# Attention in blocks of 64 queries with multiplied masks, interleaved by hand with the FFN of the chunk before

## The chip, the cores and the metric

The kernel runs on one core of a Trainium2 chip. The time is device microseconds of one execution, from a median of several runs. TensorE multiplies matrices into PSUM, VectorE (DVE) and ScalarE (ACT) read PSUM and SBUF, GpSimd (POOL) works on SBUF and issues the DMAs that cast float32 to bfloat16, SyncE (SP) issues plain DMAs.

## The reference

Eight batches, eight heads, 576 positions, head width 64. Attention is local (a query sees keys at most 32 away), and eight positions `global_idx` are global: they see all and are seen by all. The 4608 tokens of width 512 then go through a gated FFN of width 1536 with a gated residual:

```python
scores = scale * np.matmul(q, k.transpose(0, 1, 3, 2))
mask = np.abs(pos[:, None] - pos[None, :]) <= window
mask = mask | is_global[:, None] | is_global[None, :]
attn = softmax(np.where(mask, scores, -1e9))
x = np.matmul(attn, v)                      # tokens x 512
g, val = x @ w_gate, x @ w_val
ffn_out = (gelu(g) * val) @ w_out
return x + sigmoid(x @ w_res) * ffn_out
```

## The kernel before

One batch of attention is a stage of the main loop (L370). `load_batch` (L175) fetches q, k and v of the next batch in 18 casting DMAs of 96 rows on GpSimd's queue and 24 small ones for the global rows, whose addresses come from registers that all engines load at the start (L93). `transpose_batch` (L208) turns q and k with TensorE, so that a head's width lies on partitions, and ScalarE copies them out with the halos.

Per head, `qk_exp_head` (L234) computes scores of six key blocks: 96 keys and eight global keys on partitions, 160 queries and eight global queries on columns. For each block a first matmul adds the mask from `biasm` through the identity (L244, 128 rows), a second adds k times q (L246, 64 rows); then come two Exps. `av_head` (L253) multiplies with v, which carries a column of ones, so that row 64 of `nd` is the denominator. ScalarE copies numerators and denominators out.

`normalize_batch` (L273) runs after all heads of a batch: two reciprocals over 616 columns (L278), for each head two matmuls that broadcast the reciprocal over partitions (L287, L290), and three multiplies into `xt` and `xgt` (the global queries).

The FFN goes over nine chunks of 512 tokens. `piece_ff` (L309) makes one of 12 blocks of 128 FFN columns: four gate matmuls, four value matmuls, a Tanh that stands for the gelu, and two VectorE products into `ht`. `piece_st` (L328) makes 128 tokens of the output: 12 matmuls with `wo_t`, four with `wr_t`, four through the identity to bring x back in token order (L342), a Tanh, two VectorE operations and a store. The pieces wait in a list, and the loop takes one behind each head's scores and one behind each head's values (L381 to L387), so a chunk is interleaved with the attention of the next batch. What is left of the list is run before `normalize_batch`.

After the last chunk the 64 global tokens go through an FFN of their own (L407 to L439), and eight stores write them over their rows of the output (L440).

Of the kernel before, what the change touches and what calls it, by code (L numbers as in the profile page):

```python
# [8 lines left out]
_DEBUG_DUMP = False  # L9
# [5 lines left out]
AX = mybir.AxisListType  # L15
# [3 lines left out]
def kernel(  # L19
# [27 lines left out]
    PADQ = 32
    QW = PADQ + S + 32
    NDW = QW + SIDE
    NXC = NDW - PADQ  # L50
    NBIAS = -120.0
    NP = H // 2
    SHALF = 3 * BCOL
    VG = D + 2

    def sbase(kb):
        return BCOL * kb if kb < 3 else 512 + BCOL * (kb - 3)

    pieces = []
    bounds = sorted(set([BLK * kb for kb in range(KB)]  # L60
                        + [BLK * kb + WIN for kb in range(KB)] + [512, QW]))
    for i in range(len(bounds) - 1):
        c0, c1 = bounds[i], bounds[i + 1]
        if c0 >= QW:
            break
        c1 = min(c1, QW)
        kbs = [kb for kb in range(KB) if BLK * kb <= c0 and BLK * kb + WIN >= c1]
        assert kbs, (c0, c1)
        pieces.append((c0, c1, kbs))

    const = ctx.enter_context(tc.tile_pool(name="const", bufs=1))
    stage = ctx.enter_context(tc.tile_pool(name="stage", bufs=2))
    headp = ctx.enter_context(tc.tile_pool(name="headp", bufs=2))
    nump = ctx.enter_context(tc.tile_pool(name="nump", bufs=10))
    moep = ctx.enter_context(tc.tile_pool(name="moep", bufs=2))
    outp = ctx.enter_context(tc.tile_pool(name="outp", bufs=2))
    smallp = ctx.enter_context(tc.tile_pool(name="smallp", bufs=1))

    ps1 = ctx.enter_context(tc.tile_pool(name="ps1", bufs=6, space=bass.MemoryType.PSUM))
    psB = ctx.enter_context(tc.tile_pool(name="psB", bufs=1, space=bass.MemoryType.PSUM))  # L80

    ident = const.tile([128, 128], BF16, name="ident")
# [3 lines left out]
    ones64 = const.tile([128, 64], BF16, name="ones64")  # L86
    nc.vector.memset(ones64, 1.0)

    g32 = global_idx.bitcast(I32)
    gvals = []  # L90
    for i in range(NG):
        gap = bass.AP(tensor=g32.tensor, offset=g32.offset + 2 * i, ap=[[0, 1], [1, 1]])
        gvals.append(nc.values_load(gap))  # L93
    gsb = const.tile([1, NG], I32, name="gsb")
    nc.sync.dma_start(gsb, bass.AP(tensor=g32.tensor, offset=g32.offset, ap=[[0, 1], [2, NG]]))
    gf = const.tile([1, NG], F32, name="gf")
    nc.vector.tensor_copy(gf, gsb)
    gb32 = const.tile([32, NG], F32, name="gb32")
    nc.gpsimd.partition_broadcast(gb32, gf)
    diag8 = const.tile([8, NG], F32, name="diag8")  # L100
    nc.gpsimd.memset(diag8, 0.0)
    nc.gpsimd.affine_select(out=diag8, in_=diag8, pattern=[[-1, NG]], channel_multiplier=1, base=0,
                            compare_op=ALU.not_equal, fill=1.0)
    dtmp = const.tile([8, NG], F32, name="dtmp")
    nc.vector.tensor_tensor(dtmp, gb32[0:8, :], diag8, ALU.mult)
    gp8 = const.tile([8, 1], F32, name="gp8")
    nc.vector.tensor_reduce(gp8, dtmp, axis=AX.X, op=ALU.add)

    iota_i = const.tile([32, WIN], I32, name="iota_i")
    nc.gpsimd.iota(iota_i, pattern=[[1, WIN]], base=0, channel_multiplier=0)  # L110
    iotac = const.tile([32, WIN], F32, name="iotac")
    nc.vector.tensor_copy(iotac, iota_i)

    exc = const.tile([32, BCOL], F32, name="exc")
    nc.vector.memset(exc, 0.0)
    nc.vector.memset(exc[0:NG, 32:128], 1.0)

    bandf = const.tile([BLK, BCOL], F32, name="bandf")
    nc.gpsimd.memset(bandf, 0.0)
    nc.gpsimd.affine_select(out=bandf[:, 0:WIN], in_=bandf[:, 0:WIN], pattern=[[1, WIN]],  # L120
                            channel_multiplier=-1, base=0, compare_op=ALU.is_ge, fill=NBIAS)
    nc.gpsimd.affine_select(out=bandf[:, 0:WIN], in_=bandf[:, 0:WIN], pattern=[[-1, WIN]],
                            channel_multiplier=1, base=64, compare_op=ALU.is_ge, fill=NBIAS)
# [246 lines left out]
    for b in range(B):  # L370
# [19 lines left out]
        while pending:  # L390
            pending.pop(0)()
# [82 lines left out]
```

## Time and profile before

| | |
|---|---|
| median of three runs | 736.1 us (735.87 to 736.11) |
| span of the profiled execution (its time is not listed otherwise) | 729.6 us |
| TensorE busy | 85% |
| VectorE busy | 52% |
| ScalarE busy | 41% |
| GpSimd busy | 29% |
| mean granted TensorE clock | 0.916 of 2.4 GHz |

A busy TensorE is not TensorE at its peak: a matmul's recorded duration overlaps the next, and how fast the engine goes is read from start to start. Times in the rows are microseconds from the start of the span; in the lists of groups the mean is in nanoseconds.

### The profile page before, as it was taken

The numbers are of one execution on the slowest core, as the hardware profiler recorded it, in microseconds if no ns is written. First come the engines' busy times: TensorE is split into PE (matmuls) and PEld (weight loads), VectorE is DVE, ScalarE is ACT, GpSimd is POOL, SyncE is SP. The second block draws the span as 40 slices with busy tenths as digits, with TensorE's granted clock in tenths as the row PEclk, the third lists the DMA queues.
The fourth block names the chain that finished last, engine by engine and source line by source line (L and its number), as shares of the span: only waits on it lengthen the run. The fifth ranks groups of instructions, "written<-read, shape, count | busy, mean of one in ns | idle before, by whom it ended". The sixth has DMA issues, their size and how long they took to land.

```text
span 729.6 us, 11619 instructions
## 1 busy us (share of the span) xinstructions
PE 619.2 (85%) x4516; PEld 326.9 (45%) x4516; DVE 378.4 (52%) x647; ACT 301.8 (41%) x574; POOL 214.0 (29%) x353
## 2 busy tenths in 40 slices
PE   0009948998999899989999899989998999799991
PEld 0005534554555455544554455544554455244450
DVE  5702074485565636553654566355636362784740
ACT  0005445553655255525553455345544553132320
POOL 2853489804900590048003820260000000000000
PEclk9999999999799969995999599958996899799997
DMA  0909959906820691067304660240000000001010
GB/s 6 93 1 186 176 34 93 67 1 82 60 17 1 91 60 8 1 89 49 22 1 66 53 41 1 55 38 1 1 30 30 1 1 30 30 0 59 1 59 7
DMA packets 127558, 29.92 MB, mean 41 GB/s; under 512 B 119760, under 2 KB 121808, under 8 KB 127504
## 3 DMA queue, kind: packets, MB, share of 16 engines
q0 software_dynamic: 122176, 19.62, 35.4%
q1 hardware_dynamic: 5328, 9.57, 3.6%
q8 instruction: 35, 0.57, 0.3%
q14 instruction: 19, 0.16, 0.1%
HBM read 39.19 MB, written 9.57 MB: 67 GB/s over the span
## 4 chain that ended last, share of the span: by engine, by line
PE 46%; issue 28%; POOL 12%; DVE 6%; DMA 4%; POOLq 2%; ACT 1%; DVEq 0%
PE g_ps L316 10%; PE v_ps L320 9%; PE f_ps L334 7%; PE s_h L246 5%; PE s_h L244 5%; DMA wr_t<-in_moe_w_res_dram 4%; POOL ks_t L186 3%; POOL qs_t L184 3%; PE nd L259 3%; PE r_ps L338 2%; DVE xt L292 2%; POOL vt L188 2%; DVE rden L278 2%; PE pq L216 1%; PE pk L230 1%
## 5 line engine op out<-in xcount | busy, mean ns | idle before, releaser
L324 DVE SCALAR_TENSOR_TENSOR ht<-tsb,g_ps 128x512 bf16<-128x512 bf16 x108 | 73.1, 683 | 147.5 <-ACT tsb L323 147.3
L316 PE MATMUL g_ps<-xt,wg_t 128*128 128x512 bf16 x432 | 120.0, 402 | 0.3 <-DVE xt L292 0.3
L320 PE MATMUL v_ps<-xt,wv_t 128*128 128x512 bf16 x432 | 117.7, 397 | 0.0
L244 PE MATMUL s_h<-biasm,ident 128*128 128x168 bf16 x384 | 102.3, 266 | 0.0
L188 POOL DMA_DIRECT2D vt<-in_v_dram x48 | 37.1, 779 | 221.7 <-PE nd L264 214.1
L246 PE MATMUL s_h<-qte,kt 64*128 64x168 bf16 x384 | 101.0, 263 | 0.0
L334 PE MATMUL f_ps<-wo_t,ht 128*128 128x512 bf16 x432 | 99.2, 379 | 0.0
L323 ACT ACTIVATE tsb<-g_ps 128x512 bf16<-128x512 f32 x108 | 64.8, 600 | 60.1 <-PE g_ps L316 59.3
L278 DVE RECIPROCAL rden<-denb 97x616 bf16<-97x616 f32 x16 | 64.0, 4003 | 40.6 <-ACT denb L270 40.6
L325 DVE SCALAR_TENSOR_TENSOR ht<-ht,v_ps 128x512 bf16<-128x512 bf16 x108 | 73.5, 686 | 10.1 <-PE v_ps L320 1.9
L347 DVE SCALAR_TENSOR_TENSOR prb<-rsb,f_ps 128x512 f32<-128x512 bf16 x36 | 24.4, 676 | 94.2 <-ACT rsb L345 94.2
L267 ACT CAST numsb<-nd 64x616 bf16<-64x616 f32 x64 | 42.7, 667 | 68.5 <-PE nd L264 68.5
L216 PE MATMUL pq<-ident,qs_t 96*128 96x96 bf16 (+1 forms) x192 | 21.8, 281 | 57.1 <-DMA qs_t<-in_q_dram 54.7
L320 PEld LDWEIGHTS <-wv_t 128*128 128x128 bf16 x432 | 44.2, 102 | 56.9 <-issue 10.3
L218 ACT COPY qte<-pq 128x576 bf16<-128x576 bf16 x32 | 23.0, 719 | 111.2 <-PE pq L216 111.2
L334 PEld LDWEIGHTS <-ht 128*128 128x128 bf16 x432 | 40.0, 98 | 43.9 <-DVE ht L325 0.4
L345 ACT ACTIVATE rsb<-r_ps 128x512 bf16<-128x512 f32 x36 | 21.5, 598 | 91.5 <-PE r_ps L338 91.5
L246 PEld LDWEIGHTS <-kt 64*128 64x128 bf16 x384 | 36.4, 95 | 48.8 <-issue 15.0
L249 ACT ACTIVATE pt<-s_h 128x504 bf16<-128x504 f32 x64 | 39.6, 619 | 44.4 <-PE s_h L246 44.3
L259 PEld LDWEIGHTS <-vt 128*65 128x65 bf16 x1152 | 51.6, 121 | 13.3 <-issue 2.5
L259 PE MATMUL nd<-pt,vt 128*65 128x64 bf16 (+2 forms) x1152 | 54.1, 198 | 2.8 <-ACT denb L270 2.8
L244 PEld LDWEIGHTS <-ident 128*128 128x128 bf16 x384 | 38.4, 100 | 38.5 <-issue 1.5
(89 smaller groups left out, 777.2 us busy)
## 6 DMA issues: line engine op xcount, KB each, us to landing
out_dram<-ob SPq DMA_DIRECT2D x36, 256.0 KB
qs_t<-in_q_dram POOLq DMA_DIRECT2D x48, 96.0 KB, 3.7
ks_t<-in_k_dram POOLq DMA_DIRECT2D x48, 96.0 KB, 3.8
vt<-in_v_dram POOLq DMA_DIRECT2D x48, 96.0 KB, 4.2
wg_t<-in_moe_w_gate_dram POOLq DMA_DIRECT2D x1, 1536.0 KB, 10.6
wv_t<-in_moe_w_val_dram POOLq DMA_DIRECT2D x1, 1536.0 KB, 18.2
wo_t<-in_moe_w_out_dram POOLq DMA_DIRECT2D x1, 1536.0 KB, 24.9
qs_t<-in_q_dram POOLq DMA_DIRECT2D x64, 1.0 KB, 1.8
```

Source lines behind the costliest of these rows:

```text
L188: nc.gpsimd.dma_start(vt_t[0:BLK, kb, :, 0:D], vb[BLK * kb:BLK * kb + BLK])
L244: nc.tensor.matmul(sh[0:128, cb:cb + BCOL], ident, biasm[kb][0:128, 0:BCOL], start=True, stop=False)
L246: nc.tensor.matmul(sh[0:128, cb:cb + BCOL], kt[hb:hb + 64, kb, 0:128], qte[hb:hb + 64, kb, 0:BCOL], start=False, stop=True)
L259: nc.tensor.matmul(nd[0:D + 1, c0:c1], vt_t[:, kb, h, 0:D + 1], pt[:, cb + r0:cb + r0 + (c1 - c0)], start=(ii == 0), stop=(ii == len(kbs) ...
L267: nc.scalar.copy(numsb[0:D, :], nd[0:D, PADQ:NDW])
L278: nc.vector.reciprocal(rdt[0:97, :], denb_tiles[gi2][0:97, :])
L316: nc.tensor.matmul(g_ps, wg_t[:, kt2, 128 * j:128 * j + 128], xt[kt2][:, t0:t0 + 512], start=(kt2 == 0), stop=(kt2 == NKT - 1))
L320: nc.tensor.matmul(v_ps, wv_t[:, kt2, 128 * j:128 * j + 128], xt[kt2][:, t0:t0 + 512], start=(kt2 == 0), stop=(kt2 == NKT - 1))
L323: nc.scalar.activation(tsb, g_ps, ACTF.Tanh, bias=0.0, scale=0.851)
L324: nc.vector.scalar_tensor_tensor(ht[:, j, :], tsb, 1.0, g_ps, ALU.add, ALU.mult)
L325: nc.vector.scalar_tensor_tensor(ht[:, j, :], ht[:, j, :], 0.5, v_ps, ALU.mult, ALU.mult)
L334: nc.tensor.matmul(f_ps, ht[:, kt2, 128 * st:128 * st + 128], wo_t[:, kt2, :], start=(kt2 == 0), stop=(kt2 == NFF - 1))
```

## The change

The kernel is rewritten in an order fixed by hand. The 72 windows of 64 queries (nine per batch) are taken in chunks of eight, 512 tokens, so that attention and FFN chunks are the same tokens. The core, with the setup of constants left out:

```diff
+    psm = ctx.enter_context(tc.tile_pool(name="psm", bufs=4, space=bass.MemoryType.PSUM))
+    pss = ctx.enter_context(tc.tile_pool(name="pss", bufs=2, space=bass.MemoryType.PSUM))
+    psn = ctx.enter_context(tc.tile_pool(name="psn", bufs=1, space=bass.MemoryType.PSUM))
+    ctx.enter_context(tc.manual_schedule())
...
+    def load_qk(b):
+        for src, dst in ((q, q_st), (k, k_st)):
+            for r in range(NQT):
+                n = min(128, S - 128 * r)
+                nc.gpsimd.dma_start(dst[0:n, r, :].rearrange("p (h d) -> p h d", d=D),
+                                    src[b].rearrange("h s d -> s h d")[128 * r:128 * r + n])
...
+    def prep_pair(b, p, what):
+        src = q_st if what == "q" else k_st
+        ps = pss.tile([128, S], BF16, name=f"t{what}", tag="sc")
+        for r in range(NQT):
+            n = min(128, S - 128 * r)
+            nc.tensor.transpose(ps[:, 128 * r:128 * r + n], src[0:n, r, 128 * p:128 * p + 128], ident[0:n, 0:n])
+        if what == "q":
+            nc.scalar.copy(qt[b % 2][:, p, :], ps)
+        else:
+            nc.vector.tensor_copy(kt[b % 2][:, p, 32:32 + S], ps)
+    def prep_qz(b, p0, p1):
+        for u in range(2):
+            nc.vector.tensor_copy(qz[b % 2][64 * u:64 * u + 64, p0:p1, u, :],
+                                  qt[b % 2][64 * u:64 * u + 64, p0:p1, :])
+    def scores(c, quad, p):
+        sc = pss.tile([128, 4, 2, 64], F32, name="sc", tag="sc")
+        for n in range(4):
+            b, i = divmod(CH * c + 4 * quad + n, NW)
+            nc.tensor.matmul(sc[:, n, :, :], kt[b % 2][:, p, 64 * i:64 * i + 128],
+                             qz[b % 2][:, p, :, 64 * i:64 * i + 64], start=True, stop=True)
+        mine = view(pt, 0, 128, (2 * p * CH + 4 * quad) * 128, [[128, 4], [CH * 128, 2], [1, 64]])
+        nc.scalar.activation(mine, sc, ACTF.Exp, bias=0.0, scale=SCALE)
+        i0 = (CH * c + 4 * quad) % NW
+        nc.vector.tensor_tensor(mine, mine, view(maskw, 0, 128, 64 * i0, [[64, 4], [0, 2], [1, 64]]), ALU.mult)
+    def values(c, t):
+        nd = psn.tile([128, 2, 512], F32, name="nd", tag="nd")
...
+        for hf in range(2):
+            for n, (b, c0) in enumerate(parts):
+                nc.tensor.matmul(nd[:, hf, 0:HV], gt[b % 2][:, c0:c0 + 128], vgs[:, b, HV * hf:HV * hf + HV],
+                                 start=(n == 0), stop=False)
+        for h in range(H):
+            for e, (b, i) in enumerate(wins):
...
+                nc.tensor.matmul(nd[:, h // 4, VG * (h % 4):VG * (h % 4) + VG],
+                                 view(pt, 0, 128, c0, [[1, 128]]), vw,
+                                 start=False, stop=(h % 4 == 3 and e == 1))
...
+        nc.vector.reciprocal(r2, num[:, :, :, D])
+        nc.vector.tensor_tensor(xtok[c % 2][:, t, :].rearrange("p (a h d) -> p a h d", a=2, d=D),
+                                num[:, :, :, 0:D], view(rden, 0, 128, 0, [[4, 2], [1, 4], [0, D]]), ALU.mult)
+    def turn_x(c, t):
+        tx = pss.tile([128, NKT, 128], BF16, name="tx", tag="sc")
+        for kk in range(NKT):
+            nc.tensor.transpose(tx[:, kk, :], xtok[c % 2][:, t, 128 * kk:128 * kk + 128], ident)
+        nc.vector.tensor_copy(xt[c % 2][:, :, 128 * t:128 * t + 128], tx)
+    def ffn_in(c, j):
...
+        nc.scalar.activation(gsb, g_ps, ACTF.Gelu, bias=0.0, scale=1.0)
+        nc.vector.scalar_tensor_tensor(ht[:, j, :], gsb, 0.5, v_ps, ALU.mult, ALU.mult)
...
+                    nc.vector.scalar_tensor_tensor(prb, held["r"], 1.0, held["f"], ALU.add, ALU.mult)
+                    ob = work.tile([128, 512], F32, name="ob", tag="ob")
+                    nc.gpsimd.tensor_tensor(ob, prb, xtok[c % 2][:, t, :], ALU.add)
+                    r0 = 512 * c + 128 * t
+                    nc.sync.dma_start(out[r0:r0 + 128, :], ob)
...
+    for c in range(NCH):
+        b = c + 1
+        if b < B:
+            if b > 1:
+                load_v(b)
+        held = None
+        for j in range(NFF):
+            ffn_in(c, j)
+            if b < B:
+                if j < 8:
+                    prep_pair(b, j // 2, "qk"[j % 2])
+                if j == 8:
+                    shift_v(b)
+                    if b + 1 < B:
+                        load_qk(b + 1)
+                    prep_qz(b, 0, NP)
+                if j == 11:
+                    held = global_scores(b)
+        slots = {n: [] for n in range(16)}
+        if c + 1 < NCH:
+            if held is not None:
+                slots[0].append(lambda: global_exp(b, *held))
+                slots[4].append(lambda: global_rows(b))
+            for n in range(8):
+                slots[n].append(lambda n=n: scores(c + 1, n // 4, n % 4))
+            for t in range(4):
+                slots[5 + 2 * t].append(lambda t=t: values(c + 1, t))
+                slots[7 + 2 * t].insert(0, lambda t=t: turn_x(c + 1, t))
+        work_f = [w for t in range(4) for w in ffn_out(c, t)]
+        for n in range(16):
+            for w in slots[n]:
+                w()
+            work_f[n]()
```

A window has 128 keys and 64 queries of two heads, the other head's half of q being zero (`qz`). The mask, with the global keys taken out, multiplies the exponentials. Global keys and global queries get matmuls of their own: `global_scores` has eight of 288 columns and 20 of 16 columns, `global_exp` two Exps and a product, `global_rows` ten matmuls of 260 columns and a product into `vgs`. `values` takes `gt` times `vgs` into the same PSUM tile, in which a row of `gt` that is one at a global position brings in the finished numerators and denominators of that query. So the global tokens need no FFN of their own and no second store. `values` puts tokens on partitions; the residual adds x from there on GpSimd, and the four x matmuls of an output piece are gone. `ffn_out` gives four parts for each 128 tokens: the four `wr_t` matmuls with their Tanh, and three thirds of the 12 `wo_t` matmuls.

Ahead of the loop, GpSimd issues the q, k and v loads of batch 0 first, then the gate and value weights in six parts; SP loads the eight indices into its registers and gathers the global rows of all batches in 24 DMAs. VectorE zeroes the padded tiles and makes the masks. Then the preparation of batch 0 and the attention of chunk 0 run by themselves.

## Rows read from the trace of the kernel before

**Rows 1.** The page's busy time, share of the span and instructions of each engine.
```profile
PE 619.2 (85%) x4516; PEld 326.9 (45%) x4516; DVE 378.4 (52%) x647; ACT 301.8 (41%) x574; POOL 214.0 (29%) x353
```

**Rows 2.** Stages: bounds, length, busy (count) PE, PEld, DVE, ACT, POOL; PEclk, DMA, GB/s.
```profile
60.00:88.00 28.00, 28.00 (x179) 14.57 (x177) 0.00 (x0) 13.72 (x29) 7.41 (x11) 1.00 1.40 196
...
190.00:252.00 62.00, 60.13 (x472) 31.91 (x470) 33.72 (x39) 32.66 (x59) 17.24 (x26) 1.00 0.47 42
252.00:269.00 17.00, 15.23 (x84) 7.63 (x83) 8.62 (x27) 8.16 (x23) 15.22 (x27) 0.50 0.60 50
```

**Rows 3.** Timeline at the seam between two batches: start, duration, engine, line, operation.
```profile
246.91 4.00 DVE L278 RECIPROCAL rden<-denb 97x616 bf16<-97x616 f32 x1 [0.30 <-ACT denb L270]
...
248.80 0.39 PE L342 MATMUL x_ps<-ident,xt 128*128 128x128 bf16 x4
...
261.38 0.34 PE L244 MATMUL s_h<-biasm,ident 128*128 128x168 bf16 x1
...
264.44 1.89 PE L316 MATMUL g_ps<-xt,wg_t 128*128 128x512 bf16 x4
```

**Rows 4.** Timeline of TensorE at full clock, to read spacings from start to start.
```profile
193.97 0.24 PE L244 MATMUL s_h<-biasm,ident 128*128 128x168 bf16 x1
...
196.09 1.04 PE L316 MATMUL g_ps<-xt,wg_t 128*128 128x512 bf16 x4
...
244.31 0.39 PE L342 MATMUL x_ps<-ident,xt 128*128 128x128 bf16 x4
244.54 0.78 PE L259 MATMUL nd<-pt,vt 128*65 128x96 bf16 x18
...
245.35 2.75 PE L334 MATMUL f_ps<-wo_t,ht 128*128 128x512 bf16 x12
247.94 1.03 PE L338 MATMUL r_ps<-wr_t,xt 128*128 128x512 bf16 x4
...
708.32 0.28 PE L416 MATMUL vs_ps<-xgt,wv_t 128*128 128x64 bf16 x4
708.45 0.28 PE L412 MATMUL gs_ps<-xgt,wg_t 128*128 128x64 bf16 x4
```

**Rows 5.** Before the first FFN: timeline, then the load group and its time to landing.
```profile
14.69 0.26 POOL L110 IOTA iota_i<- 32x160 int32 x1 [7.15 <-issue]
...
119.52 1.89 PE L316 MATMUL g_ps<-xt,wg_t 128*128 128x512 bf16 x4
121.20 1.46 PE L320 MATMUL v_ps<-xt,wv_t 128*128 128x512 bf16 x4
...
L184 POOL DMA_DIRECT2D qs_t<-in_q_dram x48 | 37.6, 783 | 7.4 <-DMA wo_t<-in_moe_w_out_dram 7.0
...
qs_t<-in_q_dram POOLq DMA_DIRECT2D x48, 96.0 KB, 3.7
```

**Rows 6.** Timeline of the end, behind the last chunk; SPq is SP's DMA issue.
```profile
705.24 0.39 PE L342 MATMUL x_ps<-ident,xt 128*128 128x128 bf16 x4
...
716.45 10.56 SPq L443 DMA_DIRECT2D out_dram<-ogs  x8
...
726.73 0.28 SPq L443 DMA_DIRECT2D out_dram<-ogs  x1
```

**Rows 7.** Groups by line and shape: count, busy us, mean ns, idle before.
```profile
L323 ACT ACTIVATE tsb<-g_ps 128x512 bf16<-128x512 f32 x108 | 64.8, 600 | 60.1 <-PE g_ps L316 59.3
L292 DVE TENSOR_TENSOR xt<-numsb,bcA 64x512 bf16<-64x512 bf16 x64 | 43.4, 679 | 3.5 <-PE bcA L287 1.8
L249 ACT ACTIVATE pt<-s_h 128x504 bf16<-128x504 f32 x64 | 39.6, 619 | 44.4 <-PE s_h L246 44.3
L218 ACT COPY qte<-pq 128x576 bf16<-128x576 bf16 x32 | 23.0, 719 | 111.2 <-PE pq L216 111.2
L201 DVE COPY qs_t<-qs_t 8x2560 bf16<-8x2560 bf16 x8 | 11.9, 1482 | 22.6 <-DMA qs_t<-in_q_dram 22.4
L218 ACT ACT_TABLE_LOAD x1 | 1.3, 1283 | 0.9 <-PEq L458 0.9
```

More of the change, by code (lines that the diff above doesn't have):

```diff
@@ L52 @@
-    NP = H // 2
[L53 to L69, printed above, removed]
@@ L101 @@
[L101 to L110, printed above, removed]
@@ L431 @@
-    for kt2 in range(NKT):
-        nc.tensor.matmul(x_ps[0:NSG, 128 * kt2:128 * kt2 + 128], xgt[kt2][:, 0:NSG], ident,
-                         start=True, stop=True)
-    rsbs = moep.tile([128, 512], BF16, name="rsbs", tag="rsb")
-    nc.scalar.activation(rsbs[0:NSG, :], r_ps[0:NSG, :], ACTF.Tanh, bias=0.0, scale=0.5)
-    prbs = moep.tile([128, 512], F32, name="prbs", tag="prb")
-    nc.vector.scalar_tensor_tensor(prbs[0:NSG, :], rsbs[0:NSG, :], 1.0, f_ps[0:NSG, :], ALU.add, ALU.mult)
-    ogs = outp.tile([128, DM], F32, name="ogs", tag="ob")
@@ L439 @@
-    nc.vector.scalar_tensor_tensor(ogs[0:NSG, :], prbs[0:NSG, :], 0.5, x_ps[0:NSG, :], ALU.mult, ALU.add)
-    for i in range(NG):
-        dst = bass.AP(tensor=out.tensor, offset=out.offset + gvals[i] * DM,
-                      ap=[[S * DM, B], [1, DM]])
-        nc.sync.dma_start(dst, ogs[B * i:B * i + B, :])
+        gvals.append(nc.values_load(gap, engines=[mybir.EngineType.SP]))
+    for src, dst in ((k, kgf), (q, qgf)):
+        for i in range(NG):
+            rows = bass.AP(tensor=src.tensor, offset=src.offset + gvals[i] * D,
+                           ap=[[H * S * D, B], [S * D, H], [1, D]])
+            nc.sync.dma_start(dst[B * i:B * i + B, :].rearrange("p (h d) -> p h d", d=D), rows)
@@ new lines, with zero @@
+    for i in range(NG):
+        rows = bass.AP(tensor=v.tensor, offset=v.offset + gvals[i] * D,
+                       ap=[[S * D, H], [H * S * D, B], [1, D]])
+        nc.sync.dma_start(bass.AP(tensor=vgf.tensor, offset=vgf.offset + i * vgf.ap[0][0],
+                                  ap=[[NG * vgf.ap[0][0], H], [D, B], [1, D]]), rows)
+    def zero(ap):
+        nc.vector.memset(ap, 0.0)
+    for i in range(2):
+        zero(qz[i][0:64, :, 1, :])
+        zero(qz[i][64:128, :, 0, :])
+        zero(kt[i][:, :, 0:32])
+        zero(kt[i][:, :, 32 + S:64 + S])
+        if i == 0:
+            nc.vector.memset(ve[0][:, :, :, D:VG], 1.0)
+            zero(ve[0][0:32, 0, :, :])
+            zero(ve[0][96:128, 4, :, :])
+            zero(pt[:, :, :, 64:128])
+            zero(gt[0][:, 0:64])
+            zero(gt[0][:, 64 + S:128 + S])
+            zero(ptg[0][:, :, 0:64])
@@ new lines @@
+    for p in range(NP):
+        prep_pair(0, p, "q")
+        prep_pair(0, p, "k")
+        prep_qz(0, p, p + 1)
+    shift_v(0)
+    spread_vg(0, nc.vector)
+    sg, ss = global_scores(0)
+    global_exp(0, sg, ss)
+    for p in range(NP):
+        scores(0, 0, p)
+    global_rows(0)
+    for p in range(NP):
+        scores(0, 1, p)
+    load_qk(1)
+    load_v(1)
+    nc.gpsimd.dma_start(wr_t, moe_w_res.rearrange("(kt p) n -> p kt n", p=128))
+    for h0 in range(0, NFF, 6):
+        nc.gpsimd.dma_start(wo_t[:, h0:h0 + 6, :], moe_w_out.rearrange("(kt p) n -> p kt n", p=128)[:, h0:h0 + 6, :])
@@ new lines @@
+    for t in range(4):
+        values(0, t)
+        if t:
+            turn_x(0, t - 1)
+    turn_x(0, 3)
+    for b in range(1, B):
+        spread_vg(b, nc.gpsimd)
+    for c in range(NCH):
[23 more added lines that the diff above has]
+                slots[n].append(lambda n=n: scores(c + 1, n // 4, n % 4))
+            for t in range(4):
+                slots[5 + 2 * t].append(lambda t=t: values(c + 1, t))
[5 more added lines that the diff above has]
+            work_f[n]()
```

516 lines of the change are left out of this document (189 added, 327 removed).

## The prediction

> **What bounds the kernel now.** The order of reading was: busy shares, the stages, the timeline at the seams, the spacing of matmuls. TensorE is busy 85% of the span and the next engine, VectorE, 52% [rows 1]. Stage by stage this is two kinds of time. From 190.0 to 249.0 (248.80 and four matmuls of 0.057) TensorE hardly rests: one FFN chunk and one batch of attention lie interleaved [rows 2, 3]. Then VectorE starts the reciprocals of the denominators (4.00 us each, two of them), TensorE waits for them, multiplies out the broadcasts and transposes the next batch, and the next score matmul starts at 261.38. That seam also costs clock: the stretch from 252 to 269 has a granted clock of 0.50 (1.2 GHz) [rows 2], and the four gate matmuls at 264.44 are still slow. One batch is thus about 62 us at full clock, 17 at half.
>
> The busy stage adds up from spacings, start to start (a matmul's own duration overlaps the next) [rows 4]: 512 columns (247.94 - 245.35) / 12 = 0.216 us; 128 columns with 128 weight columns (244.54 - 244.31) / 4 = 0.057; the value matmuls (245.35 - 244.54) / 24 = 0.034; 64 columns with 128 weight columns (708.45 - 708.32) / 4 = 0.033, taken as 0.034. The score pairs take (196.09 - 193.97) / 12 = 0.177 each, for 168 columns that by the 512-column rate would take 0.071: mask (128 rows) and scores (64 rows) alternate, and each change of shape costs about 0.106. Sum: 160 x 0.216 + 96 x 0.177 + 192 x 0.034 + 16 x 0.057 = 34.6 + 17.0 + 6.5 + 0.9 = 59.0, as the trace has it. So at full clock only 34.6 of a batch's 74 us (190 to 264) is FFN.
>
> Before the loop: the first gate matmul starts at 119.52, and the 1.68 us to 121.20 for four of them is half clock [rows 5], though TensorE had been busy for 28.0 of 28 us from 60 to 88 [rows 2]; the view prints 1.00 there because it has no clock event before. Behind the loop: 24.4 us from the last chunk's x matmuls (705.24) to the end, for the 64 global tokens' own FFN and eight chained stores [rows 6].
>
> **The change, part by part.** *TensorE, per iteration* (one FFN chunk, and preparation, scores and values of the next):
> - FFN, unchanged but for the x matmuls, which go: 160 x 0.216 = 34.6.
> - Transposes of q and k: 8 groups of four 128-wide (0.057, the x matmuls' price) and one over 64 rows (0.034 and two changes of shape, 0.212): 8 x 0.474 = 3.8. Without the shape cost it is 2.1; both are kept.
> - Global keys and rows: 8 x 288 columns (0.122) + 20 x 16 columns (0.034) + 10 x 260 columns (0.110) = 2.8.
> - Scores: no mask matmul, K is 128 by the zero-padded q, so no change of shape: 32 x 0.057 = 1.8 in place of 17.0.
> - Values: four times two 260-column matmuls (0.110) and 16 of 65 columns (0.034), with a batch border in some: 3.2. By the 128-column row they would be 0.057 each and the sum 4.6.
> - Turning x: 16 x 0.057 = 0.9.
>
> Sum 47.1, of it 26.3 in the FFN-in half (12 blocks, transposes, global scores) and 20.8 in the interleaved half. Seven such iterations 329.7; the eighth without preparation 40.5; the ninth FFN alone 34.6: 404.8.
>
> The Trainium skill (TensorE: Matmul & The Clock Gate, Back-to-back issue gap) gives a sustained 81 ns per matmul of 128 columns when each has its weight load, and 131 ns at 512. The trace has 57 and 216 in just such streams, so the measurement decides; by 81 ns for all of the roughly 170 small matmuls an iteration would be near 53 us and the kernel near 530, an estimate from that page which the sum does not use, and the trace leaves it no chance of its own.
>
> *The seam goes.* The two 4.00 us reciprocals become four of 8 elements per partition (4.00 us / 616 is 6.5 ns an element, so about 0.1 and overhead), inside the interleave. What is late next there: values(t) must be normalised by VectorE before turn_x(t) two slots later and before values(t+1) may take the single nd buffer. TensorE has two FFN thirds and a score group in between, 2 x 0.86 + 0.23 = 1.95 us; VectorE needs up to one mask multiply (0.68), reciprocal 0.2 and multiply 0.68 [rows 7], 1.6 with hand-overs of 0.1. It fits narrowly; I charge 0.5 us per iteration. With no 12 us seam the clock should stay at 2.4 GHz.
>
> *VectorE and ScalarE beside TensorE.* VectorE in the FFN half: 12 x 0.68 (one product per block, the other is gone), four k copies 0.72, two q copies of 2304 elements (0.58 ns each by the 2560-element copy, 1.35): 14 of TensorE's 26 us [rows 7]. In the other half: eight mask multiplies at 0.30 (copy rate) to 0.68 (rate of the 512-column multiply), four times reciprocal and multiply, four x copies, four residual products, two global products, 0.68 each: 13 to 16 of 21 us. ScalarE: 12 x 0.60 + 4 x 0.72, then 8 x 0.62 + 4 x 0.60 + 1.1: 19 of 47. Neither is the sum.
>
> ScalarE's one table load now is 1.283 us [rows 7], with Exp, Tanh and copies after it. Gelu joins, and no row shows whether the table then changes. Floor: never. Ceiling: at each switch, two per iteration. Of these one sits behind gate(3)'s Tanh with three slots (3 x 0.86) to spare; the other between the last Gelu and the first Exp, where TensorE still has 0.86 + 1.7 of its own, and the second score group then waits up to 0.5 us. I take the ceiling and charge 0.5 per iteration. Eight iterations at 1.0 in all are 8.0.
>
> The Trainium skill (ScalarE: Activation LUTs, Table sets) has gelu in another set than exp and tanh and asks for batching by set: by it the ceiling holds. That speaks against this order of work; no run before shows it.
>
> *GpSimd and DMA.* Per iteration GpSimd issues 15 loads (128 rows cost 4/3 of 0.783, some 14 us) and four residual adds. Queued behind load_v, which waits for the last values of the batch that owned the buffer, are load_qk and the adds. load_qk is issued at block 8, about 17.5 us in, takes 9.4 to issue and 3.7 to land [rows 5]: 31, wanted at 47. The adds matter only in the tail. SP has the stores and two contiguous v shifts; nothing waits behind them.
>
> *Prologue.* GpSimd now waits for eight register loads until 14.69 before its first load [rows 5]; after, q and k are first: 1 + 9.4 + 3.7 = 14, v by 20. SP alone loads the registers (13 us at the same pace) and then issues 24 gathers: at 0.28 each plus address arithmetic some 11 us (chained like the eight stores of [rows 6], 1.5 each, 35): landed at 26. VectorE's masks and global v end at 28, four times k copy and q copies (1.4) at 34. Global scores at half clock 3.2, exps and product 2: 39. Eight Exps 5 and global rows 2.2 between: 46. Four values with their normalising in series, 2.7 each at half clock, 56.5. Bounds 46 (gathers and clock early) to 70. Then 4.4 us at half clock (264.44 to 269): +2.2.
>
> *Tail.* No global FFN, no chained stores: product 0.8, GpSimd add 1.2 (no row of GpSimd arithmetic this wide; VectorE's 0.68 is the floor, four times that the ceiling, and the value taken lies nearer the floor), store 0.3, landing and closing 2.9 + 1.3: 6 in place of 24.
>
> **Sum.** 56.5 + 2.2 + 404.8 + 8.0 + 6 = 477.5 of span against 729.6. The profiled execution has no time but its span; the median of 736.1 lies 6.5 above it, and the same is added: 484.
>
> **Rivals.**
> *The second half is paced by ScalarE and VectorE.* For: every score group passes TensorE, ScalarE, VectorE and a two-deep buffer shared with the transposes; VectorE is in order. Against: busy sums of at most 16 of 21 us. Price: both table loads (2.6), the global exps (1.1) and product (0.7) and 0.5 at each of four normalisings, 6.4 per iteration instead of 1.0: +43, 527. A load of 2.66 us with its drain, as the same page of the Trainium skill has it (What ACT_TABLE_LOAD costs), would add some 20; no row shows that drain.
>
> *Slower: the clock stays at 1.2 GHz.* For: from 60 to 88 TensorE streamed attention matmuls without rest, and at 121 the clock was still low. Against: at both seams shown the FFN's 512-column matmuls brought it up by 122 and 269, and it held through 62 us (190 to 252) with attention in between [rows 2]. If it fell in the interleaved half only: 8 x 20.8 more, 651. If everywhere: 404.8 more, 889. It turns slower than before once 252 of the 404.8 us of matmul work run at half clock.
>
> *The interleave does not hide the loads.* If DMA took twice as long as the issue, 18.8 us, load_qk would land at 40 of 47: no wait, so no chance of its own.
>
> *Nothing waits,* switches of shape are free and the prologue is at its lower bound: 484 - 8 - 12 - 10 = 454.
>
> **How the numbers follow.** Forecast (462 to 506) 0.72; paced by the other engines (506 to 550) 0.20; clock low in one half 0.03, everywhere 0.01; below 462 0.04. The predicted time is 484. The range 458 to 527 leaves out the slow half of the second case and both clock cases. Faster by over 0.2% (about what a measurement can tell here) 0.985, the same 0.005, slower 0.01.
>
> **What would show it.** Right: iterations of 47 to 49 us with granted clock 1.00, TensorE idle below 2 us in each, score matmuls 0.057 apart, first gate matmul at 50 to 62, some 17 table loads without TensorE waiting on them, 6 us behind the last matmul. Wrong: matmuls of 65 columns at 0.057 or more (+1.5 per iteration), long waits of TensorE for a mask multiply, tx or nd, transposes waiting for q_st, or clock 0.50 in mid-loop.

## The result, and the profile after

The median is 469.28 us (468.99 to 470.09), against 735.99 us for the kernel before in the same session: a ratio of 0.640, 95% interval 0.636 to 0.644. The forecast was 484 with a range of 458 to 527, so the time is 14.7 us below the forecast and well inside the range. The profiled execution took 470.09 us and its span is 468.3. All medians below leave out two executions that ran at a much lower granted clock: 577.6 us (mean clock 0.768) of the padded transposes and 688.33 us (0.807) of the old kernel with both edits.

The busy shares of the page (busy us, share, instructions of each engine) answer to [rows 1]:

```profile
PE 418.9 (89%) x3162; PEld 231.9 (50%) x3162; DVE 231.1 (49%) x439; ACT 176.0 (38%) x282; POOL 161.4 (34%) x185
```

The share of TensorE rose only from 85% to 89%; its busy time fell from 619 to 419 us. Of the 261 us that the span lost (729.6 to 468.3), 200 are busy time of TensorE and 61 are rest.

The stages, in the columns of [rows 2]: a piece of the prologue, two of the seven nearly equal iterations, the eighth, and the ninth with the end. Bounds are starts of first gate matmuls.

```profile
57.00:60.00 3.00, 2.04 (x23) 1.64 (x24) 1.72 (x5) 0.00 (x0) 3.00 (x5) 0.57 2.18 136
...
63.12:109.67 46.55, 46.55 (x360) 26.02 (x360) 23.28 (x43) 19.96 (x32) 16.15 (x17) 1.00 0.70 88
109.67:156.01 46.34, 46.34 (x359) 25.83 (x358) 23.73 (x44) 19.96 (x32) 17.86 (x19) 1.00 0.74 74
...
388.35:428.40 40.05, 40.05 (x281) 21.03 (x280) 19.33 (x36) 16.46 (x26) 4.89 (x4) 1.00 0.07 27
428.40:468.30 39.90, 34.70 (x161) 15.54 (x159) 11.68 (x17) 9.55 (x16) 5.76 (x5) 0.98 0.09 35
```

From 63.12 to 428.40 TensorE's busy time fills the stretches to the last digit, at a granted clock of 1.00. VectorE works 23 to 24 of 46.5 us and ScalarE 20. The seam at half clock of [rows 2, 3] has no counterpart in the loop.

The timeline of the loop on TensorE and of the end, in the columns of [rows 3]. It answers to [rows 3, 4 and 6]:

```profile
63.12 1.02 PE L331 MATMUL g_ps<-xt,wg_t 128*128 128x512 bf16 x4 [0.52 <-DVE xt L324]
...
64.85 0.52 PE L242 MATMUL tq<-ident,q_st 128*128 128x128 bf16 x5
65.30 1.04 PE L331 MATMUL g_ps<-xt,wg_t 128*128 128x512 bf16 x4
...
135.57 0.38 PE L288 MATMUL sc<-qz,kt 128*128 128x128 bf16 x4
135.79 1.03 PE L348 MATMUL r_ps<-wr_t,xt 128*128 128x512 bf16 x4
...
142.57 0.19 PE L310 MATMUL nd<-vo,pt 128*128 128x65 bf16 x1
...
143.02 0.19 PE L310 MATMUL nd<-ve,pt 128*128 128x65 bf16 x1
...
460.34 2.75 PE L358 MATMUL f_ps<-wo_t,ht 128*128 128x512 bf16 x12
```

To be read from start to start: four scores take 135.79 - 135.57 = 0.22 (0.055 each), a value matmul (142.57 to 143.02 in 15 steps) 0.030, a group of five q transposes 65.30 - 64.85 = 0.45. The last 12 matmuls end at 460.34 + 12 x 0.216 = 462.9, and 5.4 us lie behind them.

The prologue, from the timeline too (SPq is SP's issue of DMAs); it answers to [rows 5]:

```profile
17.28 7.04 SPq L150 DMA_DIRECT2D kgf<-in_k_dram  x8
18.55 0.09 DVE L167 MEMSET ve<- 128x40 bf16 x1 [14.88 <-DMA ve<-in_v_dram]
24.51 6.83 SPq L150 DMA_DIRECT2D qgf<-in_q_dram  x8
31.54 6.83 SPq L154 DMA_DIRECT2D vgf<-in_v_dram  x8
...
35.03 0.42 DVE L218 CAST kgb<-kgf 64x512 bf16<-64x512 f32 x1
...
40.35 0.42 DVE L228 CAST vgb<-vgf 64x512 bf16<-64x512 f32 x1 [0.93 <-DMA vgf<-in_v_dram]
```

Two chains end together near 40 us: SP's 24 gathers (20.7 us of issue), and VectorE's queue, which stood 14.88 us before the memset of `ve`, because a load into that tile had been issued ahead.

The groups that answer to [rows 7]: count, busy us, mean ns, idle before.

```profile
L364 POOL TENSOR_TENSOR ob<-prb,xtok 128x512 f32<-128x512 f32 x36 | 41.8, 1160 | 221.0 <-DVE prb L362 221.0
L293 DVE TENSOR_TENSOR pt<-pt,maskw 128x512 bf16<-128x512 bf16 x72 | 30.6, 425 | 26.1 <-ACT pt L291 23.4
L338 ACT ACT_TABLE_LOAD x9 | 11.5, 1283 | 0.2
L267 ACT ACT_TABLE_LOAD x7 | 9.0, 1283 | 0.1
```

And the waits of TensorE (total us, times, longest), the first and the eighth of the list. All eight lie in the prologue, and what comes behind them is 0.3 us or less:

```profile
PE isg L199 <- DVE hot L196: 30.9, 1, 30.9
...
PE g_ps L331 <- DVE xt L324: 0.5, 1, 0.5
```

### The profile page after: what moved, and what is told of

Same layout as the page of the kernel before. It is cut to its first block, busy times and chain, and to the rows that moved or that the text cites. A ratio compares the mean times of both kernels' runs of the same rounds, so it can differ in the third digit from the quotient of the medians.

```text
span 468.3 us, 7873 instructions
## 1 busy us (share of the span) xinstructions
PE 418.9 (89%) x3162; PEld 231.9 (50%) x3162; DVE 231.1 (49%) x439; ACT 176.0 (38%) x282; POOL 161.4 (34%) x185
## 4 chain that ended last, share of the span: by engine, by line
PE 62%; issue 23%; SPq 7%; POOL 4%; DVE 1%; ACT 1%; DMA 1%; POOLq 0%; DVEq 0%
PE g_ps L331 14%; PE f_ps L358 13%; PE v_ps L335 13%; PE r_ps L348 4%; SPq L145 3%; POOL ob L364 3%; PE nd L310 3%; SPq L150 3%; PE sc L288 2%; PE tq L242 2%; PE tk L242 2%; PE sn L277 2%; PE sg L257 2%; PE nd L304 2%; PE tx L323 1%
## 5 line engine op out<-in xcount | busy, mean ns | idle before, releaser
L339 DVE SCALAR_TENSOR_TENSOR ht<-gsb,v_ps 128x512 bf16<-128x512 bf16 x108 | 74.0, 687 | 115.5 <-PE v_ps L335 99.4
L364 POOL TENSOR_TENSOR ob<-prb,xtok 128x512 f32<-128x512 f32 x36 | 41.8, 1160 | 221.0 <-DVE prb L362 221.0
L338 ACT ACTIVATE gsb<-g_ps 128x512 bf16<-128x512 f32 x108 | 64.5, 597 | 125.2 <-PE g_ps L331 122.9
L89 POOL DMA_DIRECT2D q_st<-in_q_dram x40 | 33.9, 872 | 82.0 <-PE tq L242 81.2
L331 PEld LDWEIGHTS <-wg_t 128*128 128x128 bf16 x432 | 37.7, 98 | 40.4 <-issue 0.6
L291 ACT ACTIVATE pt<-sc 128x512 bf16<-128x512 f32 x72 | 42.3, 595 | 29.7 <-PE sc L288 29.7
L293 DVE TENSOR_TENSOR pt<-pt,maskw 128x512 bf16<-128x512 bf16 x72 | 30.6, 425 | 26.1 <-ACT pt L291 23.4
L348 PE MATMUL r_ps<-wr_t,xt 128*128 128x512 bf16 x144 | 37.0, 379 | 0.0
L89 POOL DMA_DIRECT2D k_st<-in_k_dram x40 | 36.4, 938 | 0.0
L97 POOL DMA_DIRECT2D ve<-in_v_dram x40 | 33.9, 873 | 0.0
```

The lines of the kernel that those rows point to most:

```text
L89: nc.gpsimd.dma_start(dst[0:n, r, :].rearrange("p (h d) -> p h d", d=D), src[b].rearrange("h s d -> s h d")[128 * r:128 * r + n])
L97: nc.gpsimd.dma_start(t[p0:p1, c, :, 0:D], v[b].rearrange("h s d -> s h d")[s0 + p0:s0 + p1])
L291: nc.scalar.activation(mine, sc, ACTF.Exp, bias=0.0, scale=SCALE)
L293: nc.vector.tensor_tensor(mine, mine, view(maskw, 0, 128, 64 * i0, [[64, 4], [0, 2], [1, 64]]), ALU.mult)
L331: nc.tensor.matmul(g_ps, wg_t[:, kk, 128 * j:128 * j + 128], x[:, kk, :], start=(kk == 0), stop=(kk == NKT - 1))
L338: nc.scalar.activation(gsb, g_ps, ACTF.Gelu, bias=0.0, scale=1.0)
```

## The experiments

**Price of a change of shape.** The fifth transpose of q and k runs over 128 rows (the upper 64 zeroed once) in place of 64, so no matmul of the loop changes shape.

```diff
+    nc.vector.memset(q_st[64:128, NQT - 1, :], 0.0)
+    nc.vector.memset(k_st[64:128, NQT - 1, :], 0.0)
...
-            nc.tensor.transpose(ps[:, 128 * r:128 * r + n], src[0:n, r, 128 * p:128 * p + 128], ident[0:n, 0:n])
+            nc.tensor.transpose(ps[:, 128 * r:128 * r + 128], src[:, r, 128 * p:128 * p + 128], ident)
...
```

> The fifth transpose of each q and k group gets 128 rows (64 of zeros) instead of 64, so TensorE never changes shape in the loop. In the changed kernel's trace a group goes 0.056 x 4, then 0.152 and 0.132 around the 64-row one, and the gate matmul behind it takes 0.227. If TensorE's own pace is the bound and a change of shape has the price of the prediction (0.106 each), a group falls by about 0.18, an iteration by 1.5 us (46.5 to 45.0), seven iterations by 10: about 459 us. If the price belongs to the small transpose itself, or something else paces the loop, it stays at 469.

Measured: 460.12 us (459.67 to 461.05), ratio 0.627 (0.622 to 0.632). Iterations went from 46.55 and 46.34 to 45.10 and 44.88, but for the first, which began with a low clock and took 46.88. In the timeline the group now ends after 111.25 - 110.97 = 0.28 instead of 0.45:

```profile
110.97 0.44 PE L243 MATMUL tq<-ident,q_st 128*128 128x128 bf16 x5
111.25 1.03 PE L332 MATMUL g_ps<-xt,wg_t 128*128 128x512 bf16 x4
```

More columns in less time: the padding gives back 0.17 to 0.18 us per group, eight groups 1.4 of the 1.46 us. As the padded transpose itself takes some 0.02 longer (0.057 for 128 columns against 0.034 for 64), the two changes of shape cost about 0.19. In this loop, where TensorE is the bound and hardly ever waits, an iteration is shorter by just these microseconds. The median fell by 9.2 of the 10.2 that seven iterations give; in the profiled execution the slow first one took 1.8 back. The run by itself leaves a rival, that a matmul over 64 rows is slow whatever stands beside it. The prologue of the changed kernel speaks against it:

```profile
38.14 0.39 PE L221 MATMUL tg<-ident,qgb 64*128 64x64 bf16 x4 [2.24 <-DVE qgb L218]
```

Four transposes over 64 rows in a row take 0.39 us together, each lasting 0.24, so they start 0.05 apart: without a change of shape there is no such price.

**Table loads.** The Gelu becomes a Tanh, so that no table is switched in the loop.

```diff
-        nc.scalar.activation(gsb, g_ps, ACTF.Gelu, bias=0.0, scale=1.0)
+        nc.scalar.activation(gsb, g_ps, ACTF.Tanh, bias=0.0, scale=1.0)
```

> The gelu is left out: a plain Tanh stands in its place, which needs no other table than Exp, so the 16 table loads in the loop (1.283 us each) should go. Theory: they are hidden in ScalarE's idle time: 469 within 1 us. Rival (table loads pace the seams between halves): 20 us less, about 449. The prediction charged 0.5 us per iteration: 465.

Measured: 470.31 us (469.37 to 472.35), ratio 0.641 (0.637 to 0.646): no difference, and iterations are 46.34 and 46.56 again. One load is left of 18:

```profile
L244 ACT ACT_TABLE_LOAD x1 | 1.3, 1283 | 0.8 <-PEq L445 0.8
```

So 17 loads of 1.283 us cost nothing that can be told from the spread: ScalarE has 26 us to spare per iteration, and the second score group does not wait.

**What the interleave is worth.** The attention of the next chunk runs first, then the 16 FFN parts; nothing else is changed.

```diff
         for n in range(16):
             for w in slots[n]:
                 w()
+        for n in range(16):
             work_f[n]()
```

> The same instructions, but the attention parts of an iteration all come before its 16 FFN parts instead of one by one between them. Theory (the interleave is what hides the chain TensorE, ScalarE, VectorE and the single nd buffer): as in the prologue, where scores to last x copy take 14.7 us for 6.4 us of matmuls, about 8 us more in each of 8 iterations, 535, and the granted clock may fall after each. Rival (the engines run ahead anyway, the hand-made order is worth little): under 480.

Measured: 534.04 us (533.01 to 538.45), ratio 0.727 (0.723 to 0.732); 64.8 us more than after, 8.1 per iteration. Two waits of TensorE that are 0.8 and 1.1 us in all without this edit, and a stretch of one iteration and a little more:

```profile
PE tx L323 <- DVE xtok L317: 35.8, 33, 1.3
PE sc L288 <- ACT pt L291: 7.0, 11, 1.3
...
108.00:165.00 57.00, 50.84 (x361) 27.85 (x363) 23.84 (x44) 20.01 (x33) 18.46 (x20) 0.94 0.60 60
```

Four normalisings of about 1.1 us per iteration stand open, the scores wait for their exponentials, and the clock falls in such a stretch (0.94). The two waits make some 41 of the 68 us by which the span is longer (536.5 against 468.3); the rest is not taken apart here. This is what the rival "paced by ScalarE and VectorE" describes. The size of its price, 6.4 per iteration, came near the 8.1, but not its make-up: it put 0.5 on each normalising and 2.6 on the table loads, which TensorE does not wait for. With the FFN parts in between none of it is paid.

**The old kernel with only the score matmul's shape mended.** In the kernel before, the score matmul takes all 128 rows of `kt` and `qte` in place of one head's 64; the scores are those of two heads added, and nothing else changes.

```diff
-                nc.tensor.matmul(sh[0:128, cb:cb + BCOL], kt[hb:hb + 64, kb, 0:128],
-                                 qte[hb:hb + 64, kb, 0:BCOL], start=False, stop=True)
+                nc.tensor.matmul(sh[0:128, cb:cb + BCOL], kt[0:128, kb, 0:128],
+                                 qte[0:128, kb, 0:BCOL], start=False, stop=True)
```

> The kernel before with one thing changed: the score matmul reads all 128 rows of k and q (both heads of a pair, so the separation of the heads is left out), as the mask matmul ahead of it does, so TensorE does not change shape between the two. Theory (each change of shape costs 0.106): 96 matmuls per batch go from 0.177 to about 0.073, 10 us per batch in eight batches: about 656 us. Rival (the spacing is the mask and score matmuls' own, or a wait on the same PSUM columns): 736, no change.

Measured: 645.88 us (644.8 to 646.95), ratio 0.879 (0.872 to 0.886). Twelve matmuls of one group, and the stretches of a seam in the columns of [rows 2]:

```profile
152.48 0.24 PE L244 MATMUL s_h<-biasm,ident 128*128 128x168 bf16 x1
...
153.28 0.24 PE L246 MATMUL s_h<-qte,kt 128*128 128x168 bf16 x1
...
170.00:171.00 1.00, 0.52 (x4) 0.13 (x3) 0.97 (x4) 0.00 (x0) 1.00 (x3) 0.93 0.54 188
171.00:180.00 9.00, 7.75 (x67) 6.09 (x66) 5.29 (x18) 4.93 (x16) 8.12 (x16) 0.50 0.08 11
180.00:181.00 1.00, 1.00 (x5) 0.45 (x4) 0.00 (x0) 1.00 (x6) 0.36 (x1) 0.50 0.36 23
181.00:182.00 1.00, 1.00 (x6) 0.44 (x5) 0.00 (x0) 1.00 (x4) 1.00 (x2) 0.95 1.18 75
```

The spacing is (153.28 - 152.48) / 11 = 0.073, against 0.177 in [rows 4]: of the 0.106 that the prediction read as the price of alternating shapes, 0.104 went with the alternation. 96 of them are 10 us per batch, 80 in eight; the other 11 are not taken apart, but the seams differ too. The one shown was at half clock for about 10.2 us, against 17 in [rows 2], and over the seven seams of either profile it was 6.8 to 10.2 us here and 10.2 to 20.5 before. This one edit is a third of the change's gain.

**The old kernel without its reciprocals**, and **both edits together**. The two reciprocals per batch become casting copies, so the output is not normalised.

```diff
-                nc.vector.reciprocal(rdt[0:97, :], denb_tiles[gi2][0:97, :])
+                nc.vector.tensor_copy(rdt[0:97, :], denb_tiles[gi2][0:97, :])
```

> The kernel before with the reciprocal of the denominators left out (a cast copy in its place, about 0.5 us for 4.0). Theory: one of the two reciprocals lies in the seam between batches, so 3.5 us in eight seams, about 708; if the shorter seam also keeps the clock up, up to 8 us more in each, 640 to 690. Rival (other seam work sets it): 730 or more.

> The kernel before with both: scores over 128 rows and no reciprocal (heads not separated, no division). If the two gains are independent they add: about 628 to 630. What is left down to the changed kernel's 469 is then the rest of the seam with its clock, the start (119.5 to 63.1) and the end (24.4 to 5.5).

Measured: 722.55 us (721.42 to 724.18), ratio 0.984 (0.976 to 0.992), a gain of under 2% and half the size expected, next to a spread of the old kernel itself from 727.44 to 737.17 us beside these runs; both together 636.70 us, ratio 0.866 (0.857 to 0.875), where 628 to 630 was expected. The timeline of a seam without reciprocals:

```profile
245.88 0.59 DVE L278 CAST rden<-denb 97x616 bf16<-97x616 f32 x1 [0.29 <-ACT denb L270]
...
247.77 0.39 PE L342 MATMUL x_ps<-ident,xt 128*128 128x128 bf16 x4
...
251.60 0.68 DVE L292 TENSOR_TENSOR xt<-numsb,bcA 64x512 bf16<-64x512 bf16 x1
252.55 0.68 DVE L292 TENSOR_TENSOR xt<-numsb,bcA 64x512 bf16<-64x512 bf16 x1
...
259.15 0.34 PE L244 MATMUL s_h<-biasm,ident 128*128 128x168 bf16 x1
```

From the last x matmuls to the next scores it is still 259.15 - 247.77 = 11.4 us (12.6 in [rows 3]): eight rounds of normalising multiplies at 0.95 us and the transposes follow, whatever the reciprocals take. So of the seam as the prediction read it, the wait for the reciprocals is worth only 1.2 us, 10 in eight. The granted clock gave nothing back at this seam: it was 0.50 from 251 to 271. The seam was a chain of many links, and the longest instruction was only its first.

**The prologue, three ways.** The edge columns and rows of `ve` are zeroed ahead of the first v load; the gathers and register loads are split over SP's and ScalarE's queues; or both.

```diff
+    for i in range(2):
+        nc.vector.memset(ve[i][:, :, :, D:VG], 1.0)
+        nc.vector.memset(ve[i][0:32, 0, :, :], 0.0)
+        nc.vector.memset(ve[i][96:128, 4, :, :], 0.0)
...
-        gvals.append(nc.values_load(gap, engines=[mybir.EngineType.SP]))
+        eng = mybir.EngineType.SP if i < 4 else mybir.EngineType.Activation
+        gvals.append(nc.values_load(gap, engines=[eng]))
+    gq = [nc.sync if i < 4 else nc.scalar for i in range(NG)]
...
```

> The memsets of v's edges and ones are put ahead of the v load of batch 0, so VectorE should not wait 14.9 us for that load at the start. Theory: the prologue is set by the gathers of the global rows on SP (last one issued at 37.7, landed at 40.3), so nothing or up to 2 us is gained: 467 to 470. Rival (VectorE's wait is on the path to the first FFN): 10 to 13 us less, about 457.

> Only the gathers change: four of the eight indices are loaded and gathered by SP, four by ScalarE's queue, so each has 4 register loads and 12 gathers where SP had 8 and 24 (17 us and 21 us in the changed kernel's trace): all landed by about 24 in place of 40. Theory (prologue set by two things side by side, gathers until 40.3 and VectorE's masks until 35.0 because its memset waits for the v load): VectorE's chain is next, kgb to vgb end at about 39, so only 1 to 3 us are gained: 466 to 468. Rival (gathers alone set it): 453.

> Split gathers and the early memsets of v's edges together. Theory: neither alone helps much, both together start the preparation of batch 0 at about 24 in place of 40.8, and the first gate matmul comes at 45 to 48 in place of 63.1: about 453 us. Rival (loads of q, k, v and weights set it, or ScalarE's queue is late for its copies): 462 or more.

Measured: 470.54 us with the memsets alone (ratio 0.642, 0.637 to 0.646), 471.44 with the split alone (0.641, 0.638 to 0.644), 460.44 with both (0.627, 0.623 to 0.630). VectorE's waits for DMAs with the memsets moved:

```profile
DVE kgb L216 <- DMA kgf<-in_k_dram: 7.9, 1, 7.9
```

with the split alone, and with both:

```profile
DVE ve L169 <- DMA ve<-in_v_dram: 16.3, 1, 16.3
```

```profile
DVE vgb L228 <- DMA vgf<-in_v_dram: 2.8, 1, 2.8
```

Each edit takes one chain away and leaves the other at 40 us, with the first gate matmul at 62.72 and 63.33; only both together move it, from 63.12 to 51.26. The expectation for the split alone (466 to 468) was a miss: it reckoned with VectorE's own chain, but let it end 1 to 3 us earlier, and the memset of `ve` then waited 16.3 us instead of 14.9. That for both (453 us, first gate matmul at 45 to 48) was a miss too: the preparation began at 25.47, near the 24 expected, but VectorE then waited 2.8 us for the gathered v rows, and the first gate matmul came 25.8 us after that start.

**The faster versions.** First, both prologue edits with the padded transpose.

> Split gathers, early memsets and the fifth transpose over 128 rows. If the start and the pace of the loop are independent the gains add: 469.3 - 16 - 9.5 = 444 us, with iterations of 45.0 us and a first gate matmul at 45 to 48. If the faster start only moves a wait into the first iteration (weights or the next batch's loads late), 450 or more.

Measured: 446.63 us (445.43 to 451.92), ratio 0.608 (0.605 to 0.611). The first gate matmul came at 50.04, where 45 to 48 was expected. In the profiled executions the gains add up: 13.1 us at the start and 10.2 in seven iterations of 45.10 and 44.88 are the 23.3 by which the span is shorter. The medians say 8.8 and 9.2 alone and 22.7 together; two of the four executions with the prologue edits alone took 462.6 and 463.2 us and two 458.3, and no trace shows why.

Then the copy of the gathered v rows goes behind the preparation of batch 0, and the last residual add to VectorE:

> The best version so far (gathers on two queues, edge columns zeroed ahead of the first v load, fifth transpose padded to 128 rows; 446.6 us, first gate matmul near 51) with two more edits: the copy of the gathered v rows on VectorE goes behind the preparation of batch 0, and the last tile's residual add goes from GpSimd to VectorE. Theory (VectorE's in-order queue in the prologue waits for the gathered v rows, landed at 29.2, while the first transposed q and k could be taken from 26.5 on): first gate matmul 2 to 3 us earlier, tail 0.5 us shorter (1.16 us of GpSimd's add against 0.68 of VectorE's), iterations as before: about 443.5 us. Rival (the gathered q and k rows gate the global scores anyway, so the preparation only waits elsewhere): first gate matmul unchanged, 446 us.

Measured: 446.09 us (443.69 to 448.34), ratio 0.606 (0.603 to 0.609), not to be told from the version before; about 443.5 was expected. The end got shorter by the 0.5 us expected (4.9 instead of 5.4 behind the last matmul). Its first values started at 38.80 instead of 41.12, as the theory had it, but the first gate matmul came at 49.16, after 50.04 in the version before: 10.4 us instead of 8.9 for the same four value blocks. A stretch of the version before, and then three of this one:

```profile
42.00:45.00 3.00, 1.10 (x22) 0.90 (x22) 1.92 (x5) 1.22 (x1) 2.69 (x4) 1.00 2.45 153
```

```profile
42.00:45.00 3.00, 2.11 (x26) 1.54 (x23) 1.67 (x5) 0.00 (x0) 2.74 (x4) 0.61 2.27 144
45.00:48.00 3.00, 1.92 (x22) 1.53 (x22) 1.71 (x5) 0.00 (x0) 3.00 (x5) 0.50 2.36 139
48.00:51.00 3.00, 2.45 (x9) 1.14 (x10) 0.74 (x2) 0.00 (x0) 3.00 (x4) 0.50 2.99 119
```

The first iteration began at the low clock too and took 46.91 instead of 45.09. So the clock took the gain back. The two executions of this version with a mean clock of 0.999 took 443.69 and 444.03 us; the other four, at 0.988 to 0.996, took 446.0 to 448.3. Hence the last experiment, which fills TensorE's waits there with matmuls that nobody reads:

```diff
+    def warm(n):
+        w = psm.tile([128, 512], F32, name="warm", tag="mm")
+        for _ in range(n):
+            nc.tensor.matmul(w, ident, view(maskw, 0, 128, 0, [[1, 512]]), start=True, stop=True)
     for t in range(4):
         values(0, t)
         if t:
             turn_x(0, t - 1)
+        warm(3 if t else 6)
     turn_x(0, 3)
+    warm(2)
```

> The version before it prepared batch 0 earlier (first values at 38.80 instead of 41.12) and still took 446.1 us: in its profiled execution the granted clock went to 0.50 from about 43 to 52, in the four value blocks of the prologue, where TensorE waits 0.81 us for VectorE in each; the two of its executions with a mean clock of 0.999 took 443.7 and 444.0 us. Here 17 matmuls of 512 columns (0.216 each), whose result nobody reads, fill these waits (six after the first value block, three after each further one, two at the end). Theory (the clock falls there because TensorE rests between the blocks): no granted clock below 1.00 from 39 to 60, first gate matmul at 38.8 + 8.9 = 47.7 instead of 49.16, first gate group 0.9 us long instead of 1.7, median 443.5 to 444.0 and no execution above 445.5. Rival (the clock falls by the time since it rose, or by the transfers that run beside it): the clock still at 0.50 there, 446 or, as the filling matmuls then take twice as long, 447.5.

Measured: 445.36 us (444.15 to 446.57), ratio 0.607 (0.604 to 0.609). The timeline and the stretches:

```profile
40.27 0.39 PE L303 MATMUL nd<-vgs,gt 128*128 128x260 bf16 x2
...
44.46 0.40 PE L303 MATMUL nd<-vgs,gt 128*128 128x260 bf16 x2 [0.16 <-DVE xtok L316]
...
49.20 1.02 PE L330 MATMUL g_ps<-xt,wg_t 128*128 128x512 bf16 x4
```

```profile
42.00:45.00 3.00, 2.73 (x40) 1.63 (x38) 1.72 (x4) 0.37 (x1) 2.54 (x4) 1.00 2.43 154
45.00:48.00 3.00, 2.79 (x43) 1.72 (x40) 1.90 (x5) 0.00 (x0) 3.00 (x5) 1.00 2.77 144
```

The clock did what was expected: no stretch below 1.00, a mean clock of 1.000 in all five executions, and the four blocks take 49.20 - 40.27 = 8.93 us. The time did not: 443.5 to 444.0 was expected, and one execution took 446.57. In the profiled one (445.49) the values began 1.5 us later than in the version before; 1.05 of it is that VectorE's cast of the gathered q rows waited for them (25.74 instead of 24.69). That one pair of profiles differs by as much as these last edits gain; the three faster versions overlap, and only that they beat 460 and 469 us is shown.

## Why the prediction was right

The sum had 477.5 us of span and the trace has 468.3; the median lies 14.7 below the forecast. By the prediction's own terms:

- **TensorE per iteration: right, 0.65 too high.** 47.1 was forecast, 46.45 is the mean of the two alternating lengths; the FFN-in half took 25.9 (26.3), the interleaved half 20.5 (20.8). The value matmuls are 0.030 apart instead of 0.034 and the 16-column ones 0.025, and each transposing group took 0.45 instead of 0.474. Eighth and ninth took 40.05 and 34.5 (40.5, 34.6). Together 5.1 of the error.
- **Stalls, 8 us charged: none.** This is the term that was wrong in the loop. The normalising "fits narrowly" was worked out with a mask multiply of 0.68; that figure was the 512-column multiply of [rows 7]; the mask multiply takes 0.425, and the wait is gone. The half microsecond for the table switch was an answer to a real load (17 that go with the Gelu, at 1.283) that lies wholly beside other work, as the Tanh run shows. The rival in which ScalarE and VectorE set the pace needs the interleave to fail; the serial run, whose waits are other than the rival's, is 8.1 longer per iteration.
- The Trainium skill (ScalarE: Activation LUTs, Table sets: the hidden batching unit) puts gelu and exp into different sets: the trace agrees, 18 loads with Gelu and one without. By the drain that the same page of the Trainium skill (What ACT_TABLE_LOAD costs) adds to each load, 17 switches would hold ScalarE by some 23 us more, an estimate from that page. The trace does not show it: the 17 loads begin 0.02 us after the end of ScalarE's instruction before, and behind the load at 409.02, the only one with work waiting, the next instruction starts 0.01 us after its end.
- The prediction's "roughly 170 small matmuls" are 198 by its own terms; no term of the sum uses that count.
- **Prologue: 63.1 instead of 58.7, by two mis-sized terms.** "24 gathers, at 0.28 each plus address arithmetic some 11 us: landed at 26": they took 20.7 us to issue (0.86 each), began at 17.3 instead of 13 and ended near 40. And "VectorE's masks end at 28" left out that a memset of `ve` stood 14.88 us behind a load into the same tile. Each alone made the prologue as long, some 12 us more than forecast. In return the rest took 22.8 us (40.35 to 63.12) against 28.5:

```profile
45.69 1.86 PE L257 MATMUL sg<-qt,kgz 128*128 128x288 bf16 x8
47.38 0.65 PE L262 MATMUL ss<-qgz,kt 128*128 128x16 bf16 x20
...
53.17 0.39 PE L304 MATMUL nd<-vgs,gt 128*128 128x260 bf16 x2
```

  From the global scores to the first values it was 53.17 - 45.69 = 7.5 us, where the prediction added global scores, Exps and global rows one behind the other to 12: they overlap. The global scores did run near half clock, (47.38 - 45.69) / 8 = 0.21 each against 0.122; the view prints 1.00 there because it has no clock event before 57, as in [rows 5]. And the 2.2 us of half clock behind 63 were not paid: the clock was low again from 57 to 61, but back at 63. That these misses all but cancel is luck.
- **Tail: 5.4 instead of 6.** GpSimd's add takes 1.16 (1.2 taken). The terms that the prediction lists add up to 6.5, not 6.
- **Around the span: 6.5 added, 1.8 measured.** 470.09 - 468.3 = 1.8. For the kernel before, runs listed with their spans have 1.7 too (736.69 over 735.0 in one, 729.76 over 728.1 in another): so the other 4.8 us were a difference between executions of the old kernel, whose mean clock is listed between 0.909 and 0.920, and not a time around the span that carries over.

The sum of these: +4.4 - 13.1 - 0.6 = -9.3 in the span, and -5.5 around it, 0.8 of them because the median lies below the profiled execution. Right was the main thing: the loop of the new kernel is TensorE's matmul spacing times its count, and in it the granted clock stays at 1.00. What the single-edit runs on the old kernel add is how the gain splits: mended shapes 91 us, the reciprocals 9 to 14. Of the rest, some 165 us, the start and the end can be read off: with both edits the old kernel's first gate matmul still came at 115.10, against 63.12, which is 52 us, and its end, 24.4 us in [rows 6], was not touched by them, against 5.4 now, 19 us. What is left, some 95 us, is the rest of the seams, the masks by matmul and the x matmuls, and no run here takes these apart further.

## What to carry to other kernels

Price a rewritten, TensorE-bound loop by start-to-start spacings of the same shapes in the old trace, with a separate price for each change of contraction rows, and charge no stall where the other engines' busy sums leave half the time free and the hand-over has a slot of slack (the serial order, with the same instructions and no slack, cost 8.1 us an iteration). The prologue deserves its own chain per queue: list what each engine's in-order queue waits for, the writes into tiles that a DMA is filling included, and expect no gain until the last of several equally long chains is shortened. After shortening it, look at the granted clock of the stretch that follows, for the gain can go there.

## What the hardware showed unexpectedly

- Two changes between 64 and 128 contraction rows, around one transpose, cost about 0.19 us (0.45 per group, against 0.28 with padding that adds 0.02 of its own), and alternating on every matmul 0.104 for each (0.177 against 0.073). Four matmuls over 64 rows in a row started 0.05 apart.
- The clock fell to its lower level (0.50, 1.2 GHz) in a stretch where TensorE waited five times, 0.5 to 1.41 us each, with value matmuls in between. With like waits it stayed at 1.00 in the profile of the version before, and it held in five of five executions once matmuls filled them. The Trainium skill (TensorE: Matmul & The Clock Gate, A second HAM failure mode: psum-queue depth-cycling) tells of a kernel of 512-column matmuls, cycling through PSUM banks, whose short rests between groups of matmuls make the clock go back and forth. The trace has a like case with smaller matmuls, in which the clock fell once, to 0.50 from 45 to 51 us. What activity keeps it up, the runs do not say.
- With denser score matmuls the half clock at the old kernel's seams lasted 6.8 to 10.2 us instead of 10.2 to 20.5.
- A gather of the prologue took 0.86 us from start to start on SP, 0.62 to 0.68 of it in the instruction that issues it; the stores of the old kernel's end, whose addresses come from registers too, had 0.28 for that instruction [rows 6]. What makes the gathers' longer, no run here takes apart.
